# An attention and mixer kernel: the first batch's token mixing in plain float32, channel-weight splits in two chains, and a list scheduler with other durations

## The chip, the cores and the metric

The kernel runs on one core of a Trainium2 chip. A core has five engines that work side by side, each through its own queue in order: TensorE (PE, with its weight loads as PEld), VectorE (DVE), ScalarE (ACT), GpSimd (POOL) and SyncE (SP), whose queue issues most of the DMA transfers. The metric is the device time of one execution in microseconds; of several executions the median is taken.

## What is computed

Eight batches, each of 576 positions, eight heads of 64. Attention is the sum of a pooled one (every four positions averaged) and a local one (a band of plus and minus three positions). Its output x, 576 by 512, goes through a mixer: a token product with ReLU and a residual, and a channel product with ReLU and a residual.

```python
def _moe_ref(x, w_tok1, w_tok2, w_ch1, w_ch2):
    xt = x.transpose(0, 2, 1)
    h = np.maximum(xt @ w_tok1, 0.0) @ w_tok2      # w_tok1 576x256, w_tok2 256x576
    u = x + h.transpose(0, 2, 1)
    h2 = np.maximum(u @ w_ch1, 0.0) @ w_ch2        # w_ch1 512x1536, w_ch2 1536x512
    return (u + h2).astype(np.float32)
...
    out_d = sm_attn(q_d, k_d, v_d)
    out_up = np.repeat(out_d, factor, axis=2)
    mask = np.abs(pos[:, None] - pos[None, :]) < factor
    scores = np.where(mask, scale * np.matmul(q, k.transpose(0, 1, 3, 2)), -1e9)
    attn = np.exp(scores - np.max(scores, axis=-1, keepdims=True))
    attn = attn / (np.sum(attn, axis=-1, keepdims=True) + 1e-09)
    return (out_up + np.matmul(attn, v)).astype(np.float32)
```

## The kernel before

**Numbers.** A product that has to be nearly exact is made of three passes over split operands (`mm3`, L114): each operand is held as a head and a remainder, and head times head, head times remainder and remainder times head are added up. For the token product the parts are reduced float32 (`W1`, `W2`, `xh`, `hid`), for the channel product float16 with a scale (`CW`, `CX`, `uh`, `h`). A split is always two instructions: ACT writes the head, DVE the remainder. The weights come in as 64-bit numbers and are put together to float32 by three instructions (`to_f32`: ACT, POOL, DVE).

**Stages of a batch.** Attention has four pooled pairs (`pooled`: scores `sd`, transposes `td`, products `ad`) and five local tiles (`local`: scores `sc`, transposes `pT`, products `av`). The pooled output `od` is written by four DMAs from ACT's queue into the rows of `vw` under the local windows (L477), so one product `av` adds both kinds, and ACT copies it out as `x` (L536; the fifth tile is `x_last`). `mix` (L556) then has four streams: `splits` makes `xh` from x; `products` runs the first token product into `t1` (L577 to L583), then the second in eight groups, two halves (`ch`) of four, each of two or three transposes of x (the residual) and the products with `W2` (L584 to L601); `takes` makes `hid` and copies each group out as `u` with its largest value (`umx`); `scaled` brings that value to all partitions (`um_t`, a transpose, and `um_b`, a broadcast) and splits u to `uh`. Then come the channel products: `first` (`c<-uh,CW`, twelve tiles of twelve matmuls for each half) and `second` (`c<-h,CX`, four tiles of 36).

**Weights.** `W1` has five pieces, `W2` four. Each channel weight has twelve tiles (`Channel.tile`): `to_f32`, a sum of squares on PE (`C_sum`), for each four tiles (`C1`) a common scale through `norms` and `everywhere`, then `parts`, the split (L276). The tiles lie in a row of buffers, `place`: tile i comes in float32 to `place[i + 1]`, and its split goes to `place[i]`, so a split can go once the tile before is split. In `First.scale` one stream does a scale and its four splits and then the next scale.

**Order.** Batch 0 and the start of batch 1 are ordered by `drive` (L155), a list scheduler at build time. Every stream is a generator of steps; a step names its engine, an estimated duration, the results it needs, and PSUM or work buffers that it takes or gives back. `drive` puts next the step that can start first by its estimate (within 0.15 us, PATIENCE, the first in the list of streams among those of the same engine), and counts 0.2 us from a step's end to its follower. Ahead of a PE step with an estimated wait it puts `junk` matmuls (`keep_busy`), until batch 0's u is split. The list's order is the string at L819: loads (L), channel evacuations (U), token weights (W), mixing (M), attention of batch 0 (A) and 1 (a), second weights (T), first weights' scales (S) and tiles (C) and so on. `drive` ends when batch 0's last output and batch 1's first `uh` are placed; what is left over goes ahead of the side work in the loop for batches 1 to 7 (L848), in which the attention and mixing of the next batch are laid between the dozens of channel products at a steady share. The engines then run these queues in order, whatever the estimates were.

## Time and profile before

| | us |
|---|---|
| three runs | 937.5, 945.24, 946.85; median 945.24 |
| the profiled execution's own time | 938.98 |
| its span, first to last instruction | 937.1 |
| PE busy in the span | 894.0 (95%) |
| DVE, ACT, POOL busy | 482.5, 297.7, 117.0 |
| HBM read and written | 54.85 MB and 9.44 MB |

The page gives one execution. A group's row reads: line, engine, operation, tile written and tiles read, partitions by elements, count, then busy us, mean ns of one, idle us ahead of it and what ended that. A timeline row begins with the start and the length in us, and what stands in brackets at its end is the idle time of that engine ahead of it, with the releaser. Matmuls overlap, so a row of n matmuls starts the next sooner than its length says; where the text counts PE time it takes start to start. Plain float32 matmuls show as two instructions for one of the program.

### The profile page before, as it was taken

The numbers are of one execution on the slowest core, as the hardware profiler recorded it, in microseconds if no ns is written. First come the engines' busy times: TensorE is split into PE (matmuls) and PEld (weight loads), VectorE is DVE, ScalarE is ACT, GpSimd is POOL, SyncE is SP. The second block draws the span as 40 slices with busy tenths as digits, with TensorE's granted clock in tenths as the row PEclk, the third lists the DMA queues.
The fourth block names the chain that finished last, engine by engine and source line by source line (L and its number), as shares of the span: only waits on it lengthen the run. The fifth ranks groups of instructions, "written<-read, shape, count | busy, mean of one in ns | idle before, by whom it ended". The sixth has DMA issues, their size and how long they took to land.

```text
span 937.1 us, 25758 instructions
## 1 busy us (share of the span) xinstructions
PE 894.0 (95%) x11407; PEld 709.8 (76%) x11413; DVE 482.5 (51%) x1174; ACT 297.7 (32%) x627; POOL 117.0 (12%) x191
## 2 busy tenths in 40 slices
PE   6779998999999999999989999999999999999998
PEld 3556877778867787787867788777977878777876
DVE  6788995437552565327552375426653275333221
ACT  2476553124141332314232241423323142422120
POOL 6350410120310003000130002200030000000000
PEclk9888999999999999999999999999999999999999
DMA  8772432510440006300170004400062000000000
GB/s 238 251 290 99 145 65 66 162 53 2 132 121 8 23 4 191 60 15 16 49 203 3 22 9 145 108 8 23 2 198 54 16 16 20 20 1 29 13 12 29
DMA packets 28222, 68.29 MB, mean 73 GB/s; under 512 B 3504, under 2 KB 14000, under 8 KB 26864
## 3 DMA queue, kind: packets, MB, share of 16 engines
q1 hardware_dynamic: 25552, 64.30, 23.2%
q10 hardware_dynamic: 2560, 2.36, 0.9%
q8 instruction: 89, 1.46, 0.7%
q14 instruction: 21, 0.17, 0.1%
HBM read 54.85 MB, written 9.44 MB: 69 GB/s over the span
## 4 chain that ended last, share of the span: by engine, by line
PE 72%; DMA 5%; DVE 3%; ACT 2%; issue 1%; SPq 0%; ACTq 0%
PE c L116 50%; PE t L116 10%; DMA qk<-in_qk_dram 4%; PE ad L463 3%; PE sc L495 2%; PE t L595 2%; PE av L531 1%; PE sd L436 1%; PE td L454 1%; DMA vw<-od 1%; PE pT L518 1%; ACT x L536 1%; DVE uh L641 1%; PE um_b L553 0%; SPq L371 0%
## 5 line engine op out<-in xcount | busy, mean ns | idle before, releaser
L116 PE MATMUL c<-uh,CW 128*128 128x256 f16 (+1 forms) x2304 | 306.4, 287 | 2.3 <-DVE u L753 1.8
L116 PE MATMUL c<-h,CX 128*128 128x256 f16 (+1 forms) x2304 | 304.5, 287 | 0.1
L116 PEld LDWEIGHTS <-CW 128*128 128x128 f16 x2304 | 219.0, 98 | 68.6 <-issue 14.7
L116 PEld LDWEIGHTS <-CX 128*128 128x128 f16 x2304 | 218.1, 98 | 58.2 <-issue 1.6
L727 DVE SCALAR_TENSOR_TENSOR h<-c,h 128x256 f16<-128x256 f32 (+1 forms) x192 | 86.7, 452 | 135.0 <-ACT h L725 134.9
L725 ACT ACTIVATE h<-c 128x256 f16<-128x256 f32 (+1 forms) x192 | 77.7, 406 | 181.4 <-PE c L116 178.3
L400 POOL TENSOR_TENSOR vr<-vr 72x256 f32<-72x256 f32 x64 | 53.0, 830 | 496.0 <-DMA vr<-in_vr_dram 494.5
L753 DVE SCALAR_TENSOR_TENSOR u<-c,io,u 128x256 f32<-128x256 f32 (+1 forms) x64 | 32.9, 514 | 100.0 <-PE c L116 100.0
L622 DVE TENSOR_REDUCE umx<-t 128x1 f32<-128x256 f32 (+1 forms) x64 | 29.2, 457 | 84.7 <-ACT u L620 76.2
L116 PE MATMUL t<-xh,W 128*128 128x512 f32 x240 | 68.9, 423 | 1.2 <-ACT x L536 1.2
L620 ACT COPY u<-t 128x256 f32<-128x256 f32 (+1 forms) x64 | 25.5, 398 | 133.3 <-PE t L116 110.5
L116 PE MATMUL t<-W,hid 128*128 128x256 f32 (+1 forms) x384 | 66.7, 308 | 0.0
L116 PEld LDWEIGHTS t<-W,hid 128*128 128x128 f32 x384 | 53.2, 189 | 0.3 <-DVE hid L609 0.3
L536 ACT COPY x<-av 128x512 f32<-128x512 f32 x32 | 18.6, 583 | 109.6 <-PE av L531 38.1
L116 PEld LDWEIGHTS t<-xh,W 128*128 128x128 f32 x240 | 44.1, 194 | 11.4 <-ACT x L536 2.0
L463 PE MATMUL ad<-vd,ptd 72*72 72x65 f32 x512 | 39.0, 229 | 7.5 <-issue 6.6
L463 PEld LDWEIGHTS ad<-vd,ptd 72*72 72x72 f32 x512 | 37.3, 146 | 8.9 <-issue 7.6
L531 PE MATMUL av<-vw,pt 47*32 47x64 f32 x2304 | 34.0, 228 | 9.5 <-DMA vw<-od 5.8
L531 PEld LDWEIGHTS av<-vw,pt 47*32 47x32 f32 x2304 | 27.7, 107 | 18.2 <-issue 5.8
L422 DVE TENSOR_REDUCE qd<-qk 128x72 f32<-128x288 f32 x64 | 25.9, 446 | 27.7 <-DMA qk<-in_qk_dram 27.6
L639 ACT ACTIVATE uh<-u,us 128x256 f16<-128x256 f32 (+1 forms) x64 | 29.7, 524 | 26.9 <-DVE us L122 19.8
L495 PEld LDWEIGHTS sc<-qk 64*32 64x32 f32 x2304 | 23.8, 105 | 12.2 <-issue 10.0
(108 smaller groups left out, 841.4 us busy)
## 6 DMA issues: line engine op xcount, KB each, us to landing
qk<-in_qk_dram SPq DMA_DIRECT2D x32, 579.0 KB
vw<-in_vw_dram SPq DMA_DIRECT2D x32, 351.0 KB
vr<-in_vr_dram SPq DMA_DIRECT2D x64, 144.0 KB
C_raw<-in_c_dram SPq DMA_DIRECT2D x16, 512.0 KB
out_dram<-u SPq DMA_DIRECT2D x32, 160.0 KB
C_raws<-in_c_dram SPq DMA_DIRECT2D x8, 512.0 KB
out_dram<-u SPq DMA_DIRECT2D x32, 128.0 KB
vw<-od ACTq DMA_DIRECT2D x32, 72.0 KB
```

The costliest lines, as they stand in the source:

```text
L116: nc.tensor.matmul(ps, lhs(a), rhs(c), start=first and i == 0, stop=last and i == 2, **kw)
L400: nc.gpsimd.tensor_add(t[:, 0:2], t[:, 0:2], t[:, 2:4])
L422: nc.vector.tensor_reduce(o, q[:, h], axis=AX.X, op=ALU.add)
L463: nc.tensor.matmul(ps[:, g, par], pt[:, par, kg, G * g:G * g + G], st.vd[:, kg, 2 * pr + par], start=kg == 0, stop=kg == 1)
L495: nc.tensor.matmul(ps[QB * j:QB * j + QB, par, WB * hp:WB * hp + WB], st.qk[hp][p, QB * g:QB * g + QB], st.qk[hp][p, S + QB * g:S + QB * g ...
L531: nc.tensor.matmul(ps[QB * j:QB * j + QB, par, D * hp:D * hp + D], pt[p, hp, QB * j:QB * j + QB], st.vw[h][p, g, D * hp:D * hp + D], start ...
L536: nc.scalar.copy(x[:n].rearrange("p hp two d -> p two hp d"), ps[:n, :, :4 * D].rearrange("p two (hp d) -> p two hp d", hp=4))
L622: nc.vector.tensor_reduce(umx[ch][:, c:c + 1], ps, axis=AX.X, op=ALU.max, apply_absolute_value=True)
L639: nc.scalar.activation(t[:, 0], st.u[ch][c], AF.Copy, scale=s)
L725: nc.scalar.activation(ht[:, 0], ps, AF.Relu)
L727: nc.vector.scalar_tensor_tensor(ht[:, 1], ps, 0.0, ht[:, 0], ALU.max, ALU.subtract)
L753: nc.vector.scalar_tensor_tensor(us[c], banks[c], io, us[c], ALU.mult, ALU.add)
```

## The change

- Batch 0's token product is made of plain float32 operands: x as it is, `W1_y` (the float32 weights, now in tiles of their own from the buffers `u1`), the hidden layer as one ReLU copy by ACT, and `W2_y`. There are no `xh` splits and no remainders of `hid` for batch 0; ten float32 matmuls stand for 30 reduced ones in the first product, sixteen for 48 in the second. Batches 1 to 7 keep the three passes.
- The W splits become streams of their own (`token_split`, w), at the end of the list; a step of batch 0's and of batch 1's `takes` waits for them, since buffers are used again.
- The splits of the channel weights leave `scale` and become two streams each (even and odd tiles). `place` gets one more buffer, and a tile comes to `place[i + 2]`.
- `drive` counts 0.12 us from a step to its follower, in place of 0.2; a dozen estimates change (two below); the list of streams becomes `LWUMSETaCDPHmQAwh`.

```diff
+PRIORITY = "LWUMSETaCDPHmQAwh"
...
-            it[2] = t + us + 0.2
+            it[2] = t + us + 0.12
...
-        yield from to_f32(raw, made["W", "raw", i])
-        y = raw.rearrange("p (n two) -> p n two", two=2)[:, :, 0].bitcast(F32)
-        yield step("A", 0.1 + n * 0.0011)
-        nc.scalar.copy(f[:, 0], y)
-        e = yield step("V", 0.08 + n * 0.0012)
-        nc.vector.tensor_tensor(f[:, 1], y, f[:, 0].bitcast(F32), ALU.subtract)
+        if i < len(TILES):
+            y = WY[i] = T([f.shape[0], n], F32, "u1", f"W1_y{i}")
+        else:
+            y = WY[i]
+        e = yield from to_f32(raw, made["W", "raw", i], lambda: u32(y))
         make(("W", "y", i), e)
         make(("W", "read", i), e)
+
+    def token_split(i, n, f):
+        yield step("A", 0.1 + n * 0.0011, ("W", "y", i), ("t1", 0, i) if i < len(TILES) else ("mixed", 0))
+        nc.scalar.copy(f[:, 0], WY[i])
+        e = yield step("V", 0.08 + n * 0.0012)
+        nc.vector.tensor_tensor(f[:, 1], WY[i], f[:, 0].bitcast(F32), ALU.subtract)
+        make(("W", "split", i), e)
...
-                for i in range(4 * q, 4 * q + 4):
-                    yield from self.parts(i)
+
+        def split(self, k):
+            for i in range(k, NF, 2):
+                yield step("A", 0.0, ("C1", "scale", i // 4))
+                yield from self.parts(i)
...
-        yield step("P", 1.0, ("q", b, 3), *([("tile", b, t - 3)] if t > 2 else []), take="gg")
+        yield step("P", 0.71, ("q", b, 3), *([("tile", b, t - 3)] if t > 2 else []), take="gg")
...
-        yield step("V", 1.2, give="gg")
+        yield step("V", 1.48, give="gg")
...
-            for t in range(NT):
+            for t in range(NT if b else 0):
                 yield step("A", 0.62, ("x", b, t), *([("over", 0, 0)] if b == 1 else []),
...
                 for f in range(2):
-                    mm3(st.acc[:, f], lambda a: W1[t][:, a, 128 * f:128 * f + 128], lambda a: st.xh[t][:, a],
-                        t == 0, t == NT - 1)
+                    if b == 0:
+                        n = TILES[t][1]
+                        nc.tensor.matmul(st.acc[:, f], WY[t][:, 128 * f:128 * f + 128], xf(t)[:n],
+                                         start=t == 0, stop=t == NT - 1)
+                    else:
+                        mm3(st.acc[:, f], lambda a: W1[t][:, a, 128 * f:128 * f + 128], lambda a: st.xh[t][:, a],
+                            t == 0, t == NT - 1)
...
                     for k in range(2):
-                        mm3(ps, lambda a: st.hid[k][:, a, 128 * c:128 * c + 128],
-                            lambda a: W2[k][:, a, s0:s0 + N], False, k == 1, skip_group_check=True)
+                        if b == 0:
+                            nc.tensor.matmul(ps, st.hid[k][:, 128 * c:128 * c + 128], W2_y[:, k, s0:s0 + N],
+                                             start=False, stop=k == 1, skip_group_check=True)
...
         def takes():
-            for f in range(2):
+            if b == 0:
+                ht = T([128, 2, 512], F32, "xh", "hid0")
+                for f in range(2):
+                    e = yield step("A", 0.6, ("t1", 0, NT - 1), give="gg>0" if f else "")
+                    nc.scalar.activation(ht[:, f], st.acc[:, f], AF.Relu)
+                    st.hid.append(ht[:, f])
+            for f in range(2 if b else 0):
...
-                    yield step("A", 0.4, ("t2", b, ch, c))
+                    yield step("A", 0.4, ("t2", b, ch, c), *[("W", "split", i) for i in range(NT if b else 1) if b < 2 and ch and c == (0 if b else 3)])
...
-        streams = [x for k in "LWUMTSaCDPHmQAh" for x in group[k]]
-        left = drive(streams, [("over", 0, 1)] + [("uh", 1, 0)] * (B > 1))
+        streams = [x for k in PRIORITY for x in group[k]]
+        left = drive(streams, [("over", 0, 1), ("C1", NF - 1)] + [("uh", 1, 0)] * (B > 1))
```

The loads stand in another order too: before, W's and C's pieces alternate on SP's queue, with vw after the first W piece; now five W1 pieces come first, then vw, six C tiles, four W2 pieces and six C tiles. Three places of the built programs follow, as their queues hold them.

First ACT's queue around batch 0's last x copy. Before (`CW` is a channel split, `C_raw` and `W_raw` the first step of putting a weight together, `xh` and `hid` the heads of batch 0's x and hidden layer):

```order
L203 ACTIVATE C_raw<-C_raw 128x512
L280 ACTIVATE CW_135<-CW_136,C_s_124 128x512
L226 CAST W_1_159<-W_raw 128x288
L203 ACTIVATE C_raw<-C_raw 128x512
L280 ACTIVATE CW_136<-CW_137,C_s_124 128x512
L536 COPY x_last_153<-av_4_980 64x2x4x64
L570 CAST xh_4_1043<-x_last_153 128x512
L280 ACTIVATE CW_137<-CW_138,C_s_124 128x512
L203 ACTIVATE C_raw<-C_raw 128x512 x2
L607 ACTIVATE hid_0_1070<-t_0_840 128x512
L203 ACTIVATE C_raw_958<-C_raw_958 128x512
L607 ACTIVATE hid_1_1085<-t_0_840 128x512
```

And now:

```order
L287 ACTIVATE CW_137<-CW_139,C_s_124 128x512
L204 ACTIVATE C_raw<-C_raw 128x512
L552 COPY x_3_979<-av_3_915 128x2x4x64
L538 COPY pt_4_960<-pT_4_955 128x256
L204 ACTIVATE C_raw<-C_raw 128x512
L234 CAST W_3_152<-W_y_501 128x256
L204 ACTIVATE C_raw<-C_raw 128x512
L552 COPY x_last_154<-av_4_1018 64x2x4x64
L204 ACTIVATE C_raw<-C_raw 128x512
L634 ACTIVATE hid_190<-t_0_805 128x512 x2
```

The casts of x are gone and the two ReLU copies follow each other; ahead of the last x copy stand the fourth x copy and the fifth tile's transposes, with channel work on both sides.

Next PE's queue at the end of batch 0's second token product, where the scale's transpose stands (`um_0_t`; `um_0_b` is the broadcast after it). Before:

```order
L547 MATMUL um_0_t<-ident,um_0_m 1x128
L595 MATMUL t_0_1_2_1191<-ident,x_2_850 128x128
L595 MATMUL t_0_1_2_1191<-ident,x_3_924 128x128
L595 MATMUL t_0_1_2_1191<-ident,x_last_153 128x128
L116 MATMUL t_0_1_2_1191<-W_0_158,hid_0_1070 128x320 x3
L116 MATMUL t_0_1_2_1191<-W_1_159,hid_1_1085 128x320 x3
L595 MATMUL t_0_1_2_1191<-ident,x_2_850 128x128
L595 MATMUL t_0_1_2_1191<-ident,x_3_924 128x128
L595 MATMUL t_0_1_2_1191<-ident,x_last_153 128x128
L116 MATMUL t_0_1_2_1191<-W_0_158,hid_0_1070 128x320 x3
L116 MATMUL t_0_1_2_1191<-W_1_159,hid_1_1085 128x320 x3
L553 MATMUL um_0_b<-um_0_m_1189,ones 128x1
```

And now:

```order
L617 MATMUL t_0_1_2_1147<-ident,x_2_896 128x128
L617 MATMUL t_0_1_2_1147<-ident,x_3_979 128x128
L617 MATMUL t_0_1_2_1147<-ident,x_last_154 128x128
L621 MATMUL t_0_1_2_1147<-W_y,hid_190 128x320 x2
L617 MATMUL t_0_1_2_1147<-ident,x_2_896 128x128
L617 MATMUL t_0_1_2_1147<-ident,x_3_979 128x128
L617 MATMUL t_0_1_2_1147<-ident,x_last_154 128x128
L621 MATMUL t_0_1_2_1147<-W_y,hid_190 128x320 x2
L563 MATMUL um_0_t<-ident,um_0_m 1x128
```

The transpose stood between the sixth and the seventh group, and the broadcast after the eighth; now the transpose comes after the eighth.

Last ACT's queue in batch 1's attention, where the pooled output goes out (`DMA vw`) and the local tiles follow (`pt` are transposed weights, `x` the results, `CX` splits of the second channel weight, `h` the channel product's hidden layer). Before:

```order
L280 ACTIVATE CX_1221<-CX_1222,C_s_132 128x512
L477 DMA vw_0_2015<-od_1888 8x9x256 x2
L477 DMA vw_1_2018<-od_1888 8x9x256 x2
L725 ACTIVATE h_1_9_2057<-c_0_1_10_2159 128x320
L280 ACTIVATE CX_1222<-CX_1222,C_s_133 128x512
L509 ACTIVATE P_108<-P_108 64x8x38
L725 ACTIVATE h_1_9_2057<-c_0_1_11_2201 128x320
L280 ACTIVATE CX_1222<-CX_1223,C_s_133 128x512
L536 COPY x_0_2292<-av_0_2220 128x2x4x64
L536 COPY x_1_2314<-av_1_2258 128x2x4x64
L522 COPY pt_2_2300<-pT_2_2295 128x512
L280 ACTIVATE CX_1223<-CX_1223,C_s_133 128x512
```

And now:

```order
L473 COPY ptd_3_2193<-td_3_2168 72x576
L493 DMA vw_0_2001<-od_1862 8x9x256 x2
L493 DMA vw_1_2004<-od_1862 8x9x256 x2
L538 COPY pt_1_2239<-pT_1_2234 128x512
L552 COPY x_0_2315<-av_0_2272 128x2x4x64
L538 COPY pt_2_2314<-pT_2_2309 128x512
L525 ACTIVATE P_108<-P_108 64x8x38
L552 COPY x_1_2385<-av_1_2317 128x2x4x64
L552 COPY x_2_2397<-av_2_2352 128x2x4x64
L538 COPY pt_3_2396<-pT_3_2391 128x512
```

The splits of the second weight and the hidden layer's heads are no longer among these rows; they stand earlier in the queue.

More of the change, by code (lines that the diff above doesn't have):

```diff
@@ L257, in tile @@
             raw = made[name, "raw"][i]
-            e = yield from to_f32(raw, made[name, "raw", i], lambda: self.place[i + 1].bitcast(U32), *needs)
+            e = yield from to_f32(raw, made[name, "raw", i], lambda: self.place[i + 2].bitcast(U32), *needs)
             make((name, "read", i), e)
-            e = yield step("P", 0.5, *([(name, "y", i - 1)] if i else []), take="m>" + name if i % 4 == 0 else "")
+            e = yield step("P", 0.28, *([(name, "y", i - 1)] if i else []), take="m>" + name if i % 4 == 0 else "")
             make((name, "y", i), e)
-            self.sums(i, self.place[i + 1].bitcast(BF16).rearrange("p (n two) -> p n two", two=2)[:, :, 1])
+            self.sums(i, self.place[i + 2].bitcast(BF16).rearrange("p (n two) -> p n two", two=2)[:, :, 1])
         def norms(self, q):
@@ L325, in scale, with split @@
                 nc.vector.tensor_mul(self.s[q], self.s[0], C1.inv[q])
-            for i in range(NF):
+            make(("C2", "scale"), made["S2"])
+        def split(self, k):
+            yield step("A", 0.0, ("C2", "scale"))
+            for i in range(k, NF, 2):
                 yield from self.parts(i)
@@ L354, in tile_ups_attention_mixer @@
     W2 = [sb.tile([128, 2, S], F32R, name=f"W2_{k}") for k in range(2)]
+    W2_y = sb.tile([128, 2, S], F32, name="W2_y")
+    WY = {len(TILES) + 2 * k + j: W2_y[:, k, HS * j:HS * j + HS] for k in range(2) for j in range(2)}
     W1_PIECES = [(u32(w1[s0:s0 + n]), 256) for s0, n in TILES]
@@ L414, in pool_q @@
     def pool_q(st, hp):
-        e = yield step("V", 1.55, at=st.at[hp])
+        e = yield step("V", 1.62, at=st.at[hp])
         if hp == 0:
@@ L430, in pooled @@
         one = "m" if b == 0 else "g"
-        yield step("P", 0.6, ("q", b, pr), *([("pair", b, pr - 2)] if pr > 1 else []), take="gg")
+        yield step("P", 0.65, ("q", b, pr), *([("pair", b, pr - 2)] if pr > 1 else []), take="gg")
         ps = P2(f"sd{b}_{pr}")
@@ L457, in pooled @@
         nc.scalar.copy(pt, ps[:G, :, :2 * Sd].rearrange("p a (k w) -> p a k w", k=2))
-        yield step("P", 1.05, ("v", b, 2 * pr + 1), take=one, give="w")
+        yield step("P", 1.2, ("v", b, 2 * pr + 1), take=one, give="w")
         ps = P1(f"ad{b}_{pr}", b)[:G, :260].rearrange("p (g h w) -> p g h w", g=2, h=2)
@@ L523, in local @@
         make(("tile", b, t), e)
-        e = yield step("P", 0.8, ("full", b), ("vw", b), take="gg")
+        e = yield step("P", 1.08, ("full", b), ("vw", b), take="gg")
         ps = P2(f"av{b}_{t}")
@@ L576, in products @@
             for t in range(NT):
-                e = yield step("P", 1.5, ("W", "y", t), ("xh", b, t), take="" if t else f"gg>{b}")
+                e = yield step("P", 1.5 if b else 1.8, *([("W", "split", t), ("xh", b, t)] if b else [("W", "y", t), ("x", 0, t)]),
+                               take="" if t else f"gg>{b}")
                 if t == 0:
@@ L586, in products @@
                 for c in range(4):
-                    e = yield step("P", 1.2, ("W", "y", NT + 3), ("hid", b),
+                    e = yield step("P", 1.2, *(("W", "split" if b else "y", NT + i) for i in range(4)), ("hid", b),
                                    *([("over", b - 1, 0)] if b and ch == 0 else []), take="" if c % 2 else f"gg>{b}")
@@ L808, in tile_ups_attention_mixer @@
         group["W"] = [token_weight(i, pieces[i][1], fin[i]) for i in range(len(pieces))]
+        group["w"] = [token_split(i, pieces[i][1], fin[i]) for i in range(len(pieces))]
         group["S"] = [C1.scale()]
+        group["E"] = [C1.split(k) for k in range(2)]
         group["C"] = [C1.tile(i) for i in range(NF)]
-        group["T"] = [second_weights()]
+        group["T"] = [second_weights(), C2.split(0), C2.split(1)]
         group["D"] = [C2.tile(i, ("C2", "places")) for i in range(NF)]
```

28 lines of the change are left out of this document (15 added, 13 removed).

## The prediction

> **What bounds the kernel now.** I read the stage table first (busy time of each engine from the start to the first channel product, to the start of batch 1's, and to the end), then the three compute engines' timelines through batch 0's mixing, and last batch 1's attention.
>
> ```profile
> 0.00:90.18 90.18, 68.85 (x965) 46.26 (x972) 69.41 (x163) 46.90 (x90) 38.27 (x68) 0.88 0.68 215
> 90.18:211.00 120.82, 116.26 (x1468) 92.56 (x1467) 78.39 (x185) 44.64 (x89) 24.77 (x38) 0.97 0.36 105
> 211.00:937.10 726.10, 708.85 (x8979) 571.01 (x8976) 334.74 (x828) 206.12 (x448) 54.01 (x85) 1.00 0.18 50
> L153 PE MATMUL busy<-junk 128*128 128x512 bf16 x67 | 21.2, 439 | 2.8 <-DVE junk L86 1.6 <-issue 0.4 <-DVE C_n_m L550 0.3
> ```
>
> The columns are the stretch, its length, then PE, weight loads, DVE, ACT, POOL busy, the granted clock, DMA share and GB/s. From 90.18 us PE is busy 825.1 of 846.9 us: whatever the edit does there, it can win few us. Before 90.18 PE is idle for 21.3 us, and its junk matmuls, which only keep the clock up, stand for some 21 us more. That stage is a chain through DVE (77% busy), ACT and the loads, and it ends when the first channel product starts. So the question is: how much earlier does the first `c<-uh` start, and does the rest still run without holes?
>
> The stage's last steps, PE first, then what PE waits for:
>
> ```profile
> 51.10 2.21 PE L116 MATMUL t<-xh,W 128*128 128x512 f32 x6
> 60.53 0.65 PE L531 MATMUL av<-vw,pt 47*32 47x64 f32 x32
> 66.35 0.61 PE L293 MATMUL C_sum<-CW 128*128 128x128 bf16 x4 [3.10 <-DVE CW L208]
> 68.38 3.18 PE L116 MATMUL t<-xh,W 128*128 128x512 f32 x6
> 74.14 0.39 PE L595 MATMUL t<-ident,x 128*128 128x128 f32 x2
> 74.28 0.95 PE L116 MATMUL t<-W,hid 128*128 128x256 f32 x6
> 80.97 0.27 PE L547 MATMUL um_t<-ident,um_m 128*1 128x128 f32 x1 [0.31 <-DVE um_m L544]
> 83.59 0.38 PE L553 MATMUL um_b<-um_m,ones 1*128 1x1 f32 x2
> 90.18 2.76 PE L116 MATMUL c<-uh,CW 128*128 128x256 f16 x12
> 45.79 0.57 ACT L536 COPY x<-av 128x512 f32<-128x512 f32 x1
> 65.54 0.56 ACT L536 COPY x_last<-av 64x512 f32<-64x512 f32 x1
> 67.88 1.13 DVE L572 TENSOR_TENSOR xh<-x_last,xh 128x512 fp32r<-128x512 f32 x1
> 72.95 0.60 ACT L607 ACTIVATE hid<-t 128x512 fp32r<-128x512 f32 x1 [0.19 <-DVE hid L609]
> 73.63 0.67 DVE L609 SCALAR_TENSOR_TENSOR hid<-t,hid 128x512 fp32r<-128x512 f32 x1
> ```
>
> PE has the last attention tile at 61.2, but ACT copies it out at 65.54, because three channel-weight splits stand ahead in its queue. DVE gives the split's second half at 69.0, the product runs 68.38 to 71.4 (at a low clock: 3.18 us for six passes), and the hidden layer leaves DVE at 74.24. The second mixing product starts at 74.14, its scale's transpose at 80.97, and the channel product 9.2 us later.
>
> **The change, part by part.** The sum is made against this execution (938.98 us, span 937.1); the median of the three runs is 945.24, so this one is a low run, and I carry the difference over to the median.
>
> *Plain float32 in batch 0.* Removed from the chain: batch 0's x splits (an ACT and a DVE instruction for each tile) and DVE's two hidden splits. Between the last x copy's end (66.10) and the second product (74.14) lie 8.04 us. What stays of them is one product of two float32 matmuls and two ACT copies (0.60 and 0.50 start to start). The price of a float32 matmul of 512 columns isn't in the trace; the nearest rows:
>
> ```profile
> L463 PE MATMUL ad<-vd,ptd 72*72 72x65 f32 x160 | 12.7, 232 | 7.5 <-issue 6.6 <-ACT ptd L457 0.4 <-DVE od L471 0.3
> L436 PE MATMUL sd<-qd 64*72 64x144 f32 x96 | 9.6, 310 | 0.5 <-DVE qd L424 0.5
> L116 PE MATMUL t<-xh,W 128*128 128x512 f32 x60 | 18.9, 452 | 0.0
> 53.37 1.64 PE L116 MATMUL t<-xh,W 128*128 128x512 f32 x6
> 15.48 1.25 PE L463 MATMUL ad<-vd,ptd 72*72 72x65 f32 x16
> 16.66 0.78 PE L495 MATMUL sc<-qk 64*32 64x38 f32 x64
> ```
>
> `ad` and `sd` are plain float32, and the trace has two instructions for each of the program's. From 65 to 144 columns one grows by 78 ns, 0.99 ns a column, so 512 columns cost 2 x 0.51 = 1.01 us. The bounds: 0.5 us if float32 streamed like the reduced form (six passes in about 1.6 us, 0.26 each, twice), and 1.15 us by `ad`'s start-to-start time (1.18 us for 16 of 65 columns, 1.13 ns a column). I take 1.01, nearest to the row with most columns. The Trainium skill (FP8 and Floating Point Precision, TensorE Precision Notes) says that true FP32 takes four passes through the array, and the split form here has three; by that, an estimate of 4 x 0.26 = 1.04 us, the edit makes PE's share a third dearer. It agrees with the slope of these rows, and no run here shows a 512-column one.
>
> So the last product is 2.0 us, the two copies 1.1, hops 0.3: 3.4 in place of 8.04, **-4.6**. The other four products sit in PE's idle time between the x tiles.
>
> *When the last x arrives.* Its rows are the pieces of weight work:
>
> ```profile
> 68.02 1.22 ACT L203 ACTIVATE C_raw<-C_raw 128x512 f32<-128x512 f32 x2
> L203 ACT ACTIVATE C_raw<-C_raw 128x512 f32<-128x512 f32 x16 | 10.6, 672 | 0.0
> L280 ACT ACTIVATE CW<-CW,C_s 128x512 f16<-128x512 f32 x12 | 8.6, 721 | 3.6 <-DVE C_s L274 2.0 <-DVE CW L282 1.5
> L208 DVE SCALAR_TENSOR_TENSOR W_raw<-W_raw 128x256 uint32<-128x256 uint32 x4 | 1.7, 416 | 0.0
> L226 ACT CAST W<-W_raw 128x256 fp32r<-128x256 f32 x4 | 1.7, 420 | 5.2 <-DMA vw<-od 4.6 <-DVE W_raw L208 0.5
> L228 DVE TENSOR_TENSOR W<-W_raw,W 128x256 fp32r<-128x256 f32 x4 | 2.2, 540 | 1.9 <-ACT W L226 1.9
> ```
>
> Two preludes take 1.22 where each has 0.67: neighbours overlap by 0.07 to 0.12, and I count from start to start. Five `W_y` (0.35 each) now stand on DVE ahead of the fourth pooled pair's reduce, so the pooled output and the first `av` come some 1.7 us later: +1.7. On ACT 19.75 us pass from the first x copy (45.79) to the last (65.54); the new order has there seven C preludes (0.6), four of W2 and four casts (0.35), four channel splits (0.65), four x and three pt copies (0.5, from the 0.57 of a copy): 13.1 us. It also waits for the third transpose behind two float32 products on PE (2.3), and for the scale of the first weights and two `av` (some 1.5): 16.9. 1.7 - 2.85 = **-1.1**. Second product at 74.14 - 4.6 - 1.1 = 68.4. The loads are no bound there: the same bytes stand ahead of the sixth C tile.
>
> *Second product and scale.* A group transposes two or three x pieces (0.07 each, 74.14 to 74.28) and adds two float32 matmuls, of 256 columns (0.51) or 320 (0.63): four of 1.15 and four of 1.47, 10.5 us. PE now has all eight ahead of the scale's transpose, which stood after six: 68.4 + 10.5 = 78.9, against 80.97. From there it took 9.21 us to the channel product, with two groups of 1.21 between transpose and broadcast (80.97 to 83.59). These are gone from that place: 9.2 - 2.4 = 6.8, so the channel product starts at 85.7 against 90.18: **-4.5**. The stage is then DVE's again (scale, four `uh` splits among C2's preludes).
>
> *Two chains, later W splits.* ACT no longer waits for DVE between one tile's halves; the nine W splits (0.54 on DVE, as above) leave the front, four before the product and five in batch 1's attention. That is the cover which makes the x copies above early, and is counted there: 0 more.
>
> *Batch 1's attention.* Its rows:
>
> ```profile
> 140.93 1.22 PE L463 MATMUL ad<-vd,ptd 72*72 72x65 f32 x16 [0.23 <-PE sc L495]
> 141.99 1.79 PE L116 MATMUL c<-uh,CW 128*128 128x320 f16 x12
> 143.63 1.47 PE L116 MATMUL c<-h,CX 128*128 128x256 f16 x12
> 144.94 1.79 PE L116 MATMUL c<-uh,CW 128*128 128x320 f16 x12
> 147.15 0.27 PE L531 MATMUL av<-vw,pt 47*32 47x64 f32 x2 [0.42 <-DMA vw<-od]
> 148.03 1.52 PE L531 MATMUL av<-vw,pt 47*32 47x64 f32 x126 [0.61 <-DMA vw<-od]
> 154.76 1.19 PE L531 MATMUL av<-vw,pt 47*32 47x64 f32 x64 [1.26 <-ACT pt L522]
> 149.48 0.66 PE L518 MATMUL pT<-ident,P 128*128 128x128 f32 x4
> ```
>
> From the last `ad`'s end (142.0) to `av`'s second half (148.03) the pooled output needs 6.0 us, 5.2 to the first. In the new order only two dozens of products (1.31 us a dozen, 143.63 to 144.94), a transposed tile (0.66) and the half-size last scores (0.39, half of the row at 16.66) cover it: 3.7 us, where three dozens did 4.7. PE waits 2.3 here against 1.03: +1.3. The later wait of 1.26 for `pt` behind C2 splits on ACT goes, since no split stands there now: -1.26. W's five late splits (2.7 us) delay the fifth tile on DVE behind three `av` of cover. Net 0, bounds -2 and +3 (the waits of 1.03 and 1.26 gone, or the first one twice as long again).
>
> *Later batches.* The same products, with the side work one dozen products later. The longest kind of wait there is DVE's, held up by loads (between batches 1 and 3):
>
> ```profile
> 260.75 1.79 PE L116 MATMUL c<-uh,CW 128*128 128x320 f16 x12 [1.52 <-DVE u L753]
> ```
>
> It may go, or another come: 0, bounds of 2 each way. One dozen stays between scale and the next batch's first product, as batch 2 had it before.
>
> Sum: -4.5; 938.98 becomes 934.5, and the median 945.24 - 4.5 = **941** in round numbers.
>
> **The rivals.**
> (a) *No gain.* The transpose behind all eight groups eats what the hidden layer won: with float32 at 1.15 us and one more us of waiting for x, the second product starts at 69.7, takes 11.8, and the channel product starts at 88.3; with +2 in the attention the change is 0: 945. For it: PE must run through all eight groups by its order. Against: it needs both terms at their bad end.
> (b) *Slower: the mixing runs at half clock.* Rows at 68.38 (3.18 us, where 53.37 has 1.64) show it after a 3.1 us wait for DVE. If the second product ran wholly so, it would take 21.0, and the channel product start at 96.2, +6: 951. It decides above 15 us of second product. Against: before, it began three us after that slow row and had full speed (0.95 for six at 74.28); the new order has junk matmuls ahead of it too. The Trainium skill (TensorE: Matmul & The Clock Gate, Part 1) has the array at half clock after an idle window of about 3.4 us and at full after a busy one; the two rows agree with a factor of two.
> (c) *More gain.* The first stage's longest hole is PE's own:
>
> ```profile
> 24.80 0.87 PE L463 MATMUL ad<-vd,ptd 72*72 72x65 f32 x6 [6.57 <-issue]
> ```
>
> It waits for nothing the profile names, in the middle of a row of equal matmuls, while DMA is full. With other loads queued there it may be shorter; without it all is 6.5 earlier, with the sum above 934. It can as well be longer.
>
> **How the numbers follow.** The forecast (channel product 1 to 7 us earlier) has 0.58, (a) 0.17, (b) 0.07, (c) 0.18. The three runs of before lie from 937.5 to 946.85, and a median can fall at either end. The range reaches to (c) with a low run and past (a): 931 to 949. A measurement of this kernel can tell about 1% (9.5 us) from no change. Faster by more needs (c), or the forecast with low runs: 0.26; slower needs (b) with high runs: 0.07; between: 0.67.
>
> **What would show it.** In the profile after: no `xh` for batch 0; float32 `t` in two instructions of about 0.5 us (512 columns); last x copy near 64.5, second product at 68.4, scale's transpose at 78.9, first `c<-uh` at 86; in batch 1 a wait of 2 to 3 us at the first `av`. If the first `c<-uh` isn't before 89, the float32 price or ACT's queue is wrong; if it is early and the time isn't, the holes after it are. If the first hole on PE moves by more than 3 us, the start isn't the change's doing alone.

## The result and the profile after

| | before | changed |
|---|---|---|
| median, us | 943.14 (937.5 to 946.85, 4 runs) | 933.09 (930.35 to 936.33, 4 runs) |
| ratio, 95% interval | | 0.989 (0.9842 to 0.9938) |
| once more, beside the first experiments | 942.87 (934.01 to 954.14) | 933.16 (931.82 to 938.12); 0.990 (0.9865 to 0.9935) |
| profiled execution, span | 937.1 | 931.9 |

The change makes the kernel about 1% faster: 10 us between the medians, 5.2 us between the two profiled executions, since the one of before is a low run of its kernel. The profiles can explain only the 5.2 us; the rest lies in executions that no profile shows.

The stage table of the changed kernel, cut where the channel products of batches 0, 1 and 2 begin (the 1st, 577th and 1153rd row of PE that writes `c`; a batch has 576). The columns are those of the prediction's first table.

```profile
0.00:89.20 89.20, 71.91 (x955) 44.37 (x964) 66.31 (x154) 42.60 (x85) 34.05 (x68) 0.92 0.75 231
89.20:204.01 114.81, 109.79 (x1440) 88.79 (x1439) 79.06 (x188) 45.54 (x89) 20.35 (x34) 1.00 0.34 94
204.01:312.66 108.65, 105.71 (x1404) 85.82 (x1404) 52.34 (x129) 31.58 (x68) 13.73 (x21) 1.00 0.23 65
312.66:931.90 619.24, 605.22 (x7600) 487.67 (x7597) 285.36 (x700) 175.40 (x381) 42.44 (x68) 1.00 0.17 48
```

The kernel before, cut at the same products (its first stage stands in the prediction):

```profile
90.18:207.51 117.33, 112.77 (x1442) 90.41 (x1441) 75.78 (x178) 42.58 (x84) 24.77 (x38) 0.97 0.37 108
207.51:317.90 110.39, 107.81 (x1407) 86.00 (x1407) 54.64 (x136) 33.66 (x74) 9.78 (x17) 1.00 0.21 59
317.90:937.10 619.20, 604.52 (x7600) 487.15 (x7597) 282.71 (x700) 174.52 (x380) 44.23 (x68) 1.00 0.17 48
```

Between these two executions the first stage is 1.0 us shorter, batch 0's channel stage 2.5, batch 1's 1.7, and the 619 us from batch 2 on are equal to 0.04 us. In batch 0's channel stage PE is idle for no less (114.81 - 109.79 = 5.0 us, 4.6 before), but its granted clock is 1.00 in place of 0.97. The split into stages is that of one execution each: the second profile of the changed kernel (span 930.0, in the table of all runs below) has its first stage 0.3 us longer than before, the next two 5.0 and 2.5 shorter, and the rest 0.1 longer. What both have in common is a gain of 4 to 8 us between the first channel products of batches 0 and 2.

PE's timeline in the first stage of the changed kernel (start, length, operation; the wait ahead in brackets), for the rows that the prediction named:

```profile
20.62 1.22 PE L479 MATMUL ad<-vd,ptd 72*72 72x65 f32 x8 [1.98 <-issue]
...
42.79 0.27 PE L547 MATMUL av<-vw,pt 47*32 47x64 f32 x2 [3.06 <-DMA vw<-od]
45.14 1.17 PE L547 MATMUL av<-vw,pt 47*32 47x64 f32 x62 [2.08 <-DMA vw<-od]
...
55.89 1.98 PE L600 MATMUL t<-x,W_y 128*128 128x512 f32 x4
57.80 0.38 PE L569 MATMUL C_n_b<-C_n_m,ones 1*128 1x1 f32 x2
...
67.84 1.98 PE L600 MATMUL t<-x_last,W_y 64*128 64x512 f32 x4
...
70.81 0.38 PE L617 MATMUL t<-ident,x 128*128 128x128 f32 x2
...
76.09 0.41 PE L617 MATMUL t<-ident,x 128*128 128x128 f32 x2 [0.79 <-DVE umx L654]
...
81.75 0.27 PE L563 MATMUL um_t<-ident,um_m 128*1 128x128 f32 x1
...
89.20 1.47 PE L117 MATMUL c<-uh,CW 128*128 128x256 f16 x12
```

A tile's two float32 matmuls take 57.80 - 55.89 = 1.91 us, so 0.95 each. The second product starts at 70.81 and the first channel product at 89.20, forecast for 68.4 and 85.7. The first dozen of channel products takes 1.47 us, where before it took 2.76.

ACT's timeline shows why x is late. The first row is its DMA queue:

```profile
36.33 7.75 ACTq L493 DMA_DIRECT2D vw<-od  x4
44.13 1.20 ACT L204 ACTIVATE C_raw<-C_raw 128x512 f32<-128x512 f32 x2 [8.68 <-DMA vw<-od]
...
46.40 0.59 ACT L552 COPY x<-av 128x512 f32<-128x512 f32 x1 [0.73 <-PE av L547]
...
53.62 0.59 ACT L538 COPY pt<-pT 128x512 f32<-128x512 f32 x1 [3.11 <-PE pT L534]
...
58.80 1.33 ACT L287 ACTIVATE CW<-CW,C_s 128x512 f16<-128x512 f32 x2 [1.27 <-DVE C_s L281]
60.04 0.68 ACT L204 ACTIVATE C_raw<-C_raw 128x512 f32<-128x512 f32 x1
61.21 1.38 ACT L287 ACTIVATE CW<-CW,C_s 128x512 f16<-128x512 f32 x2 [0.49 <-DVE CW L289]
62.50 0.65 ACT L204 ACTIVATE C_raw<-C_raw 128x512 f32<-128x512 f32 x1
63.05 0.57 ACT L552 COPY x<-av 128x512 f32<-128x512 f32 x1
...
66.99 0.58 ACT L552 COPY x_last<-av 64x512 f32<-64x512 f32 x1 [1.65 <-PE av L547]
```

The same row of the kernel before:

```profile
37.83 3.44 ACTq L477 DMA_DIRECT2D vw<-od  x4
```

The hole of 6.57 us in `ad` is 1.98 us now, and the pooled output is there 1.5 us earlier (36.33 against 37.83). But its four copies take 7.75 us to issue in place of 3.44, and ACT stands still for them. Later the fourth x copy stands behind four channel splits until 63.05. The last copy is at 66.99; before it was at 65.54.

### The profile page after: what moved, and what is told of

It is laid out like the page before. It is cut to its first block, busy times and chain, and to the rows that moved or that the text cites. A ratio compares the mean times of both kernels' runs of the same rounds, so it can differ in the third digit from the quotient of the medians.

```text
span 931.9 us, 25737 instructions
## 1 busy us (share of the span) xinstructions
PE 892.6 (96%) x11393; PEld 706.6 (76%) x11401; DVE 483.1 (52%) x1167; ACT 295.1 (32%) x622; POOL 110.6 (12%) x191
## 4 chain that ended last, share of the span: by engine, by line
PE 86%; DMA 6%; DVE 3%; ACT 2%; issue 2%; POOL 1%; SPq 0%; ACTq 0%; POOLq 0%
PE c L117 57%; PE t L117 10%; DMA vw<-od 4%; PE ad L479 3%; PE av L547 3%; PE sc L511 2%; PE sd L452 2%; PE t L617 2%; PE td L470 2%; PE pT L534 1%; DMA qk<-in_qk_dram 1%; PE t L600 1%; DMA vr<-in_vr_dram 1%; DMA C_raws<-in_c_dram 1%; ACT x L552 1%
## 5 line engine op out<-in xcount | busy, mean ns | idle before, releaser
L416 POOL TENSOR_TENSOR vr<-vr 72x256 f32<-72x256 f32 x64 | 50.5, 789 | 485.2 <-ACT ptd L473 250.6
L654 DVE TENSOR_REDUCE umx<-t 128x1 f32<-128x256 f32 (+1 forms) x64 | 29.3, 457 | 84.9 <-ACT u L652 63.3
L117 PE MATMUL t<-W,hid 128*128 128x256 f32 (+1 forms) x336 | 58.0, 308 | 0.0
L117 PE MATMUL t<-xh,W 128*128 128x512 f32 x210 | 57.9, 412 | 0.0
L117 PEld LDWEIGHTS t<-W,hid 128*128 128x128 f32 x336 | 46.4, 189 | 0.0
L117 PEld LDWEIGHTS t<-xh,W 128*128 128x128 f32 x210 | 37.8, 188 | 7.8
```

Source lines behind the costliest of these rows:

```text
L117: nc.tensor.matmul(ps, lhs(a), rhs(c), start=first and i == 0, stop=last and i == 2, **kw)
L416: nc.gpsimd.tensor_add(t[:, 0:2], t[:, 0:2], t[:, 2:4])
L654: nc.vector.tensor_reduce(umx[ch][:, c:c + 1], ps, axis=AX.X, op=ALU.max, apply_absolute_value=True)
```

## The experiments

Ratios are against the kernel before, with 95% intervals; a stage or a start is read from the one profile of each kernel. The first three kernels have one part of the change each. A hop is what `drive` counts from a step to its follower.

**Float32 alone.** Of the diff: batch 0's products and `takes`, `token_weight` and `token_split`, and the list with w at its end.

```diff
-        streams = [x for k in "LWUMTSaCDPHmQAh" for x in group[k]]
+        streams = [x for k in "LWUMTSaCDPHmQAwh" for x in group[k]]
```

> The kernel before, with batch 0's mixing in plain float32 and the token weights split late, and nothing else: one chain of channel splits, the planner's old durations and its old hop of 0.2. Theory A (the float32 mixing carries the gain: no x splits, no hidden splits on the way to the second product): ratio 0.990 to 0.995 against before, second product of batch 0 starts at 69 to 72 us. Theory B (the durations carry it, because the order that they give keeps PE's clock up and takes waits away behind the first stage): ratio 0.997 to 1.005, although the second product may start early. Theory C (run-to-run luck with the loads of the first 25 us): no part alone differs from before by more than 0.3%.

0.9941 (0.9916 to 0.9966), as theory A has it; the second product starts at 65.96, earlier than its 69 to 72. The first channel product starts at 86.5, 3.6 us earlier: the forecast's -4.5 nearly. But batch 0's channel stage takes 121.6 us against 117.3, and the profiled execution (span 941.2) is the highest of its twelve.

**Planner's numbers alone.** Of the diff: the dozen durations and the hop.

```diff
-            it[2] = t + us + 0.2
+            it[2] = t + us + 0.12
```

> The kernel before, with the planner's new durations and the hop of 0.12 and nothing else; each instruction is the same, only the order in which the engines have them differs. Theory A: ratio 0.997 to 1.005. Theory B: ratio 0.990 to 0.995, with batch 0's second product still at 73 to 75 us, and the first channel products at full clock. Theory C: within 0.3% of before.

1.0045 (1.0017 to 1.0074): slower, against theory B. The first channel product starts 3.0 us later (93.2), and, unlike in the changed kernel, the stretch from batch 2 on takes 628.2 us against 619.2.

**Two chains alone.** Of the diff: `place` with a buffer more, the streams `split`, S and E ahead of T in the list, and `drive` ending only when the first weight's last tile is split too.

```diff
-                for i in range(4 * q, 4 * q + 4):
-                    yield from self.parts(i)
+        def split(self, k):
+            for i in range(k, NF, 2):
+                yield step("A", 0.0, ("C1", "scale", i // 4))
+                yield from self.parts(i)
```

> The kernel before, with the channel weights' splits in two chains and nothing else. Both theory A and theory B: ratio 0.997 to 1.003 (prediction: 0 us). A rival for this part alone: ACT no longer waits for DVE between two splits, so splits crowd the x copies less, and the last x copy of batch 0 moves from 65.5 to 63 or 64 us: ratio 0.995.

0.9943 (0.992 to 0.9966): the rival's 0.995. The last x copy stands at 63.47 (65.54). The first channel product is later all the same (92.2), and the profile, with a span of 937.5, doesn't show the gain that the medians do (939.0 against 942.87).

**The changed kernel again.**

> The changed kernel once more, for a closer ratio and a second profile. Ratio 0.987 to 0.993. The second profile tells what is constant: theory C has the first hole of PE (in the pooled scores, near 20 to 25 us) at another length by more than 2 us, with the first channel product moved by as much; theories A and B have the first channel product at 88 to 90 us whatever that hole is.

0.990. The first hole on PE is 2.99 us, and all up to the first channel product some 1.3 us later (90.5). In the three kernels with one part it is 6.61, 1.81 and 6.57 us. So theory C falls as a cause of the ratio: float32 and the chains each gain 0.6% with the long hole in their profile, the planner's numbers lose with the short one.

**Without the planner's part.** Float32 and chains together; the durations and the hop are the old ones.

> The changed kernel with the planner's old durations and the old hop of 0.2: float32 mixing and two chains only. If the parts add (0.9941 for float32, 0.9943 for the chains, 1.0045 for the planner, each alone): 0.9885, 1 to 4 us below the changed kernel, with the loads in the old order (the values' windows ahead of all token weights but the first), no wait of ACT between the four copies of the pooled output, and the first channel product at 86 to 89 us. Rival (the parts don't add, the new durations are needed where the two others change the work): 0.993 to 0.995, since float32 and the chains then take out the same waits.

0.994 (0.9907 to 0.9972): the sum of the parts, 0.9885, lies outside, so they don't add. Against the changed kernel (0.9842 to 0.9938, and 0.9865 to 0.9935) the intervals overlap: whether the planner's numbers add a gain to these two parts is unclear. The four copies go out without a break, as expected. The first channel product starts at 82.6, 6.6 us ahead of the changed kernel, and at batch 2's the lead is 0.5 us (312.2 against 312.7). Its PE rows there show what becomes of an early start:

```profile
81.75 0.61 PE L299 MATMUL C_sum<-CW 128*128 128x128 bf16 x4 [2.88 <-DVE CW L208]
...
82.57 2.45 PE L116 MATMUL c<-uh,CW 128*128 128x256 f16 x12
```

A wait of 2.88 us, and the first dozen runs 2.45 us in place of 1.47.

**Without float32.** Chains and planner's numbers.

> The changed kernel without the float32 mixing: two chains and the planner's new numbers only. If the parts add: 0.9988, the first channel product at 92 to 95 us (93.2 with the planner's numbers alone, 92.2 with the chains alone). Rival: the gain of the changed kernel is that of the chains with the planner, 0.991 to 0.993, with float32 worth next to nothing in that order.

1.0072 (1.003 to 1.0114): neither expectation. The first channel product is at 98.9, and the stretch from batch 2 on 626.1 us.

**The windows' loads first**, in the changed kernel:

```diff
-        group["L"] = [pool_all(st), load_v(st), weight_loads(pieces, "h", "W"), windows(st)]
+        group["L"] = [pool_all(st), load_v(st), windows(st), weight_loads(pieces, "h", "W")]
```

> The changed kernel with one line of the stream list moved: the loads of the values' windows stand ahead of the token weights' loads. Theory: with the hop of 0.12 below the patience of 0.15, the five token weights go ahead of the windows, these land late, ACT's third copy of the pooled output waits for that (4.4 us between the second and the third issue), and so does av (3.06 and 2.08 us). Then here: the four copies are issued without a break, av's two waits sum to 3 us at most, the last mixing product of the first kind starts at 65.5 to 66.5 (67.84), the first channel product at 87 to 88 (89.2), and the time is 1 to 2.5 us below the changed kernel. Rival: the windows land by the bytes ahead of av, whatever their order; then the waits are of the same length and the first channel product within 0.5 us of 89.2 to 90.5.

0.988 (0.9825 to 0.9934), span 927.0. The first channel product is at 87.4 and `av` waits 0.93 us, as expected, and the last mixing product of the first kind is at 63.29, earlier than expected; but the copies are still broken, so the reason given was wrong (what breaks them stands below, with the old hop):

```profile
36.05 6.26 ACTq L493 DMA_DIRECT2D vw<-od  x4
```

**The same, and the channel splits held until batch 0's last x copy.**

```diff
-                yield step("A", 0.0, ("C1", "scale", i // 4))
+                yield step("A", 0.0, ("C1", "scale", i // 4), ("x", 0, len(TILES) - 1))
```

> As the run before, and with the channel weights' splits held until batch 0's last x copy. Theory (ACT's queue holds x back: the fourth x copy stands at 63.05 though its product on PE was done at 58.97, behind four splits): the last product of the first kind at 62 to 64, the second mixing product at 65 to 67, the first channel product at 85 to 87.5, 2 to 4 us below the changed kernel. Rival: DVE is full until the first channel product, so what is held comes back there: the second mixing product is early, but the first channel product stays at 87 to 90 and the time is that of the run before, or the channel products then wait for splits.

The last x copy comes at 59.6 and the first channel product at 84.4, earlier than the theory asked. The time is no better: 0.9939 (0.9902 to 0.9976) against 0.988 (0.9825 to 0.9934), intervals that just overlap. In the profile, a high execution of this kernel (span 938.5), batch 0's channel stage takes 120.7 us (111.4 with the windows first alone), and the stretch from batch 2 on 626.7 against 620.5.

**No junk between the mixing's first products and the first channel product**, in the changed kernel:

```diff
-            if e == "P" and ("uh", 0, 1) not in made and free["g"]:
+            if e == "P" and ("t1", 0, 4) not in made and free["g"]:
```

> The changed kernel without the junk matmuls that PE has between the mixing's first kind of products and the first channel product (15 of 87 rows of junk in the order; none of them adds to the output). Theory (a share of the gain is the granted clock: in the kernel before the first dozen of channel products took 2.76 us, with the planner's order and its junk 1.47): the first dozen takes 2.3 to 2.8 us again, the granted clock of the 8 us around it falls to about 0.8, and the time is 1 to 3 us above the changed kernel (0.992 to 0.993). Rival: PE has enough sums and transposes there to keep the clock, or the junk holds the path up; then the first dozen stays at 1.5 us and the time is that of the changed kernel (0.990) or less.

The clock falls as expected:

```profile
87.63 0.40 PE L322 MATMUL C_sum<-CX 128*128 128x128 bf16 x4 [1.80 <-DVE CX L209]
87.87 2.52 PE L117 MATMUL c<-uh,CW 128*128 128x256 f16 x12
90.19 0.42 PE L563 MATMUL um_t<-ident,um_m 128*1 128x128 f32 x1
90.40 2.03 PE L117 MATMUL c<-uh,CW 128*128 128x256 f16 x12
```

but no rise of the time is shown: 0.9916 (0.9882 to 0.995) holds both the 0.990 of the changed kernel and the 0.992 to 0.993 of the theory, and the profile's span is 927.0. With `um_t` at the same time (81.78, and 81.75 in the changed kernel) the channel product starts 1.3 us earlier, the first dozen is through at 90.2, there at 90.5, and the third starts at 92.7, there at 92.4. The junk costs here nearly what it keeps up.

**More junk in the kernel without the planner's part** (nine matmuls, most ahead of the `C_sum` quoted above):

```diff
-                keep_busy(min(8, int((t - clock["P"]) * 0.6 / 0.22)))
+                keep_busy(min(16 if ("u", 0, 0) in made else 8, int((t - clock["P"]) * (1.2 if ("u", 0, 0) in made else 0.6) / 0.22)))
```

> Float32 mixing and two chains on the planner's old numbers (the run without the planner's part), with 9 more junk matmuls ahead of the first channel product, and nothing else. In that run the first channel product came 6.6 us ahead of the changed kernel's (82.6 against 89.2) but its dozen took 2.45 us behind a wait of 2.88, and the time was no better. Theory: the early start is eaten by the clock and by batch 1's attention; with the junk the first dozen takes 1.5 us and the time falls by 1 to 2 us (0.992). Rival: the junk stands in the way (a late C_sum, a later first channel product), or what is won at 83 us is lost at batch 1's attention, where the clock falls once more near 152 us: 0.994 as before.

The first dozen is at full clock (1.47 us), but starts at 84.9 and not 82.6. 0.9906 (0.9872 to 0.9941) against 0.994: the intervals overlap, so that it gains is unclear.

**The old hop with the new durations.**

```diff
-            it[2] = t + us + 0.12
+            it[2] = t + us + 0.2
```

> The changed kernel with the hop of 0.2 in place of 0.12, all durations as changed. With 0.2 above the patience of 0.15 the loads stand in the old order again (the windows behind the first token weight). If the load order is what the planner's part costs: no break between the copies of the pooled output, the first channel product at 83 to 88 us, and a ratio of 0.986 to 0.990. Rival: the durations cost it; then ratio and first channel product are those of the changed kernel, 0.990 and 89 to 91 us.

0.991 (0.9874 to 0.9947), the rival's ratio, with the theory's first channel product (84.5). The profiled execution is the lowest of its twelve. The copies are broken worse than ever, though the windows are loaded early:

```profile
32.64 8.85 ACTq L493 DMA_DIRECT2D vw<-od  x4
```

So the order of the windows' loads is not what breaks them. The loads of SP and the copies of ACT take eight semaphores in turn, in the planner's order. In the changed kernel the third copy has by that the semaphore of the first, and waits for it (`DMAHW2` in ACT's queue):

```
L493 DMA vw_0_217<-od_356 8x9x256 [waits DMAHW2_49,DVE_49]
L493 DMA vw_0_217<-od_356 8x9x256
L493 DMA vw_1_220<-od_356 8x9x256 [waits DMAHW2_49]
L493 DMA vw_1_220<-od_356 8x9x256 [waits DMAHW4_49]
```

The third copy goes out when the first has landed. The semaphore events in the traces say so: in the changed kernel the last event of the first copy is at 42.65 us and the third copy starts at 42.67; with the old hop it is 40.05 and 40.07, with the windows first 40.89 and 40.91. In all seven profiles with a break the first and the third copy share a semaphore; in the seven without one the four copies have four. No run changed that by itself.

**One chain in the changed kernel.** Float32 and planner's numbers.

> The changed kernel with one chain of channel splits: float32 mixing and the planner's new numbers only. Theory (two chains and float32 take out the same waits of ACT, so that with float32 the second chain adds next to nothing): 0.990 to 0.993, first channel product at 88 to 91 us. Rival (with the planner's numbers each of the two is needed, as without float32 they gave 1.0072): 0.997 to 1.002.

1.007 (1.0035 to 1.0104): beyond both. The first channel product is early (84.6), but batch 0's channel stage takes 122.2 us, and from batch 2 on:

```profile
316.24:943.30 627.06, 608.47 (x7600) 488.47 (x7597) 281.21 (x700) 176.52 (x380) 37.75 (x68) 1.00 0.16 47
```

The stretch has as many matmuls and weight loads as the changed kernel's (x7600, x7597) and is 7.8 us longer; PE's idle time in it is 18.6 us against 14.0, and the other 3.2 us lie in PE's busy time. From 320 to 880 us its longest wait of PE by total is one that the changed kernel doesn't have there (who waited for whom, us in total, times, longest):

```profile
PE sc L503 <- DVE pd L452: 5.5, 10, 0.6
```

The same 5.5 us stand there with the planner's numbers alone and without float32, and 2.2 us with the splits held.

**All runs side by side.** Starts of the first channel product of batches 0, 1 and 2, the stretch from there to the end, and the span, worked out from the traces as for the stage tables:

| kernel | ratio | batch 0 | batch 1 | batch 2 | to the end | span |
|---|---|---|---|---|---|---|
| before | 1 | 90.2 | 207.5 | 317.9 | 619.2 | 937.1 |
| float32 | 0.9941 | 86.5 | 208.2 | 319.4 | 621.9 | 941.2 |
| chains | 0.9943 | 92.2 | 208.2 | 318.2 | 619.3 | 937.5 |
| float32, chains | 0.994 | 82.6 | 202.2 | 312.2 | 618.6 | 930.7 |
| the same, more junk | 0.9906 | 84.9 | 202.2 | 311.3 | 619.1 | 930.4 |
| changed | 0.989 | 89.2 | 204.0 | 312.7 | 619.2 | 931.9 |
| changed, again | 0.990 | 90.5 | 202.8 | 310.7 | 619.3 | 930.0 |
| changed, no late junk | 0.9916 | 87.9 | 200.7 | 307.8 | 619.2 | 927.0 |
| changed, windows first | 0.988 | 87.4 | 198.8 | 306.6 | 620.5 | 927.0 |
| changed, old hop | 0.991 | 84.5 | 197.8 | 308.2 | 615.7 | 923.9 |
| planner | 1.0045 | 93.2 | 208.2 | 316.5 | 628.2 | 944.7 |
| planner, chains | 1.0072 | 98.9 | 209.4 | 317.9 | 626.1 | 944.0 |
| planner, float32 | 1.007 | 84.6 | 206.8 | 316.2 | 627.0 | 943.3 |
| windows first, splits held | 0.9939 | 84.4 | 205.1 | 311.8 | 626.7 | 938.5 |

Two things stand in it. The first channel product's start says little of the time: it ranges over 16 us and doesn't sort the ratios. And the last stretch has two lengths, 616 to 622 and 626 to 628 us. From batch 2 on all these kernels do the same work, and PE's order repeats from batch to batch; in the traces of the last four kernels it is another one. Counted in dozens of channel products from a batch's first, their last pooled product `ad` comes at 17 and the first two groups of `av` at 20.9 and 23.0; in the others `ad` is at 18 (19 with the old hop) and `av` at 21.6 and 24.0 (22.6 and 24.8). With the first order goes a stretch that is some 8 us longer, 0.85% of the time; without it the three with the planner's numbers would stand at 0.996, 0.9987 and 0.9985 and the one with the splits held at 0.9854, by this sum. No run moved that order by itself, so that it costs the 8 us is read from fourteen profiles without an exception, not shown by an edit, and which of its rows would cost them stays open.

The kernel with the windows' loads first has the lowest ratio, but its interval overlaps the changed kernel's: below before for sure, below the change unclear.

## Why the prediction was right or wrong

The forecast was 941 us, 4.5 below before, which counts as no clear change; measured were 933.09, within the range, and a change of 1.0 to 1.1%, on the edge of what can be told from none and of rival (c). On the profiled execution it was -4.5, measured -5.2. That these two are near is luck: the forecast's whole gain was to stand at the first channel product, which came 1.0 us earlier, and 0.3 us later in the second profile, and what was measured lies in the stages after it, which the sum had at 0.

- *Float32 in batch 0: right.* 0.95 us a matmul, forecast 1.01; from the last x copy's end (66.99 + 0.58) to the second product 3.2 us, forecast 3.4. The Trainium skill (FP8 and Floating Point Precision, TensorE Precision Notes) gives four passes, an estimate of 1.04 us: within a tenth. PE's share is dearer by a fifth (1.98 us for a tile's two results, 1.64 in the split form), not by a third. Alone the part moves the first channel product by -3.6.
- *When the last x arrives: wrong by 2.5 us*, forecast -1.1, measured +1.45. The start of the stretch did not fail: the first x copy came at 46.40, 0.6 us later where the sum had 1.7, although the pooled output's copies held ACT up for 7.75 us in place of 3.44, for which the sum has no term. What failed is the stretch from the first to the last x copy, 16.9 us in the sum and 20.6 in the trace, and in it the waits: ACT's work is 12.9 us (forecast 13.1), its waits are 7.7 (forecast 2.3 and 1.5). They are 3.1 for the third transpose, 2.8 for three `av` (0.47, 0.66, 1.65), and 1.27 and 0.49 ahead of the splits, which come as a block ahead of the fourth x and the last `pt`.
- *Second product and scale: right in length.* 10.9 us from 70.81 to `um_t`, forecast 10.5 (0.79 of it a wait); 7.5 from there, forecast 6.8. So the first channel product was 1.0 us early and not 4.5: as the text had it for a start after 89, ACT's queue.
- *Two chains: "0 more" failed.* Alone they gain 0.6%, and the changed kernel without them is slower than before.
- *Batch 1's attention: right on the waits.* They were to be net 0 and are 2.7 us (0.98, 0.51 and 1.24, rows below) against 2.3 before; the wait for `pt` went, as forecast, and the 1.24 is one of those of the last section. But the clock is missing in the sum. Before:

```profile
154.76 1.19 PE L531 MATMUL av<-vw,pt 47*32 47x64 f32 x64 [1.26 <-ACT pt L522]
...
156.50 2.28 PE L116 MATMUL c<-h,CX 128*128 128x256 f16 x12
```

 and in the changed kernel:

```profile
154.77 0.27 PE L547 MATMUL av<-vw,pt 47*32 47x64 f32 x2 [0.98 <-DMA vw<-od]
155.55 0.84 PE L547 MATMUL av<-vw,pt 47*32 47x64 f32 x62 [0.51 <-DMA vw<-od]
...
159.98 0.60 PE L534 MATMUL pT<-ident,P 128*128 128x128 f32 x4 [1.24 <-issue]
160.41 1.47 PE L117 MATMUL c<-h,CX 128*128 128x256 f16 x12
```

 Before had two stretches at a low clock in this stage, the changed kernel has none (views of 8 us of before; the clock is the third number from the right):

```profile
88.00:96.00 8.00, 7.55 (x51) 5.37 (x51) 6.51 (x20) 3.29 (x6) 0.00 (x0) 0.79 0.67 224
152.00:160.00 8.00, 6.74 (x187) 5.24 (x186) 2.05 (x4) 3.73 (x7) 0.00 (x0) 0.79 0.02 4
```

 At 0.79 over 8 us a stretch loses 1.7 us, two lose 3.4: the stage's 2.5 us and the 0.5 us more of idle time, nearly. It is no free gain, since the run without late junk has one of the two again and a time that can't be told from the changed kernel's.
- *Later batches: right*, 619.2 us before and after. But the bound of 2 us was too narrow for what the order can do there: the planner's numbers with only one of the other parts cost 7 to 8 us.
- *The rivals.* (b) did not come. Of (a) the landmark came, and by another way: the channel product starts at 89.2, later than the 88.3 that (a) had, because x is late and not because of float32's price; its 2 us in the attention and its time did not come. (c)'s mechanism came, the hole is 4.6 us shorter, and was worth 1.5 us at the pooled output and none behind the copies. With holes of 6.6, 5.3 and none (float32 alone, with chains, old hop) the first channel product starts at 86.5, 82.6 and 84.5.

Where the 5.2 us of this pair of profiles lie: 1.0 us in the first stage, where PE is idle 4.0 us less (21.3 to 17.3; 3.9 of it are the waits of the last section, 8.0 before and 4.2 now) and busy 3.1 us more, 2.3 of it junk (21.2 us before):

```profile
L154 PE MATMUL busy<-junk 128*128 128x512 bf16 x79 | 23.5, 416 | 2.7 <-DVE junk L87 1.6 <-DVE C_n_m L566 0.4 <-DVE C_inv L278 0.2
```

then 2.5 us in batch 0's channel stage, where the clock no longer falls, and 1.7 us in batch 1's; the order shifts work between the two. Which part of the change keeps the clock up is not shown: with the two chains alone it is up as well, without a gain in the stages to batch 2 (318.2 against 317.9).

## What to carry to other kernels

A scheduler's estimates act far from where they were measured: first see which order the steady part runs in, since here it has two lengths 8 us apart, and judge an edit of the start with that held equal. An earlier landmark is no gain until the next one has moved as well; give the start of every stage, not of one. A transfer that an engine issues can hold that engine up for as long as an earlier one takes to land, if both have the same semaphore: look up which ones share. Two edits that are each worth 0.6% can be worth 0.6% together, and be the difference between loss and gain beside a third.

## What was not expected of the hardware

The granted clock fell without a long wait. Before, it is down at 156.5 behind waits of at most 1.26 us between small `av` products, and in the run without junk behind one of 1.80:

```profile
88.00:96.00 8.00, 8.00 (x61) 6.30 (x59) 6.59 (x17) 4.57 (x10) 0.01 (x1) 0.79 0.29 87
```

With half a clock for what it lost, 0.21 x 8 / 0.5 makes 3.4 us, and the same 0.79 stands in the two views of the kernel before. The clock records of the traces have it so: half a clock for 3.41 us from 89.91 and from 154.76 before, and from 88.11 in the run without late junk. In the 3.41 us ahead of each PE was not idle but busy for 69%, 58% and 32%. The Trainium skill (TensorE: Matmul & The Clock Gate, Part 1) has windows of 3.4 us that put the clock to half after an idle one; the length agrees, the idle window does not, as no wait in these three places comes near 3.4 us.

PE's hole in the first `ad` products, which waits for nothing that the views name, is by the traces a wait for PE's own program, the next block of its instructions. The page of the changed kernel has these two lines (before, the second is the same):

```profile
PE 892.6 (96%) x11393; PEld 706.6 (76%) x11401; DVE 483.1 (52%) x1167; ACT 295.1 (32%) x622; POOL 110.6 (12%) x191
q8 instruction: 89, 1.46, 0.7%
```

PE's 22794 rows are 256 for each of these 89 transfers of 16 KB. In the twelve profiles that have the hole (0.6 to 6.6 us) it stands at the same place of PE's queue, 448 to 450 rows from its start with the sequencer's counted, and later waits of this kind stand 256 rows or a multiple of that further on (706, 962, 2753). PE goes on 1.3 to 1.8 us after such a transfer has ended: before, the transfer runs from 21.69 to 23.13 us and PE goes on at 24.80; in the changed kernel from 17.54 to 19.02, and PE goes on at 20.62. With the old hop and without float32 it has ended by 17.07 and 16.46, and there is no such hole. So the length of the hole depends on when the next block of instructions comes through, while the DMA engines are 96 to 99% busy (10 to 30 us, before); what sets that time stays open, and the hole goes neither with the order of the loads (6.6 us before and none with the old hop, 2.0 and 4.1 with W's pieces or the windows first) nor with the start of the channel products. No run moved such a transfer by itself. Such waits make 3.4 us of batch 0's channel stage in the first profile of the changed kernel (2.18 and 1.24) and 1.1 in the second, which is most of the 2.5 us that the two differ by in that stage.
